# Attention and two dense layers on one core: a sign of its own for each row, and wide weight splits made in two pieces

## The chip, the cores and the metric

The kernel runs on one core of a Trainium2 chip. A core has TensorE (PE in the profile, with PEld for its weight loads), VectorE (DVE), ScalarE (ACT), GpSimd (POOL) and SyncE (SP), which here only issues DMAs. The metric is the time of one execution in device microseconds; the median of several runs is compared.

## The reference

The inputs are q, k and v of shape (4, 12, 448, 64), two gain vectors, and the weights of two dense layers. All are float32.

```python
q_n, k_n = rmsnorm(q, g_q), rmsnorm(k, g_k)
scores = q_n @ k_n.T / 8                      # per batch and head
attn = softmax(scores); x = attn @ v          # regrouped to 1792 tokens x 768
h = x @ moe_w_in                              # 768 x 2048
x = (h * sigmoid(1.702 * h)) @ moe_w_out      # 2048 x 768
h = x @ moe2_w_in                             # 768 x 2048
g = maximum(h, 0) + alpha * minimum(h, 0)     # alpha: 2048 values, drawn from 0 to 0.3
out = g @ moe2_w_out                          # 2048 x 768
```

## The kernel before, in words

Float32 operands of the large products are held as two float16 parts, a rounded high part and the remainder, and each product is made of three float16 matmuls (high by high, high by low, low by high). Weights are scaled by a power of two per row ahead of that, so that both parts fit float16.

**Weights.** `weights` (L202) loads a weight matrix in rows of 128. A row of the input weights is 2048 columns wide and comes in four loads; `from_words` turns the loaded words into numbers on ScalarE (L148) and VectorE (L164, L165). Then VectorE takes the row's largest magnitude (L245), and `row_scales` makes the scale of the row (L172 is its last instruction). `split_rows` (L177) writes the high part on ScalarE (L179) and the low part on VectorE (L180). There are 6 such rows for `moe_w_in` (tile `w1i`) and 6 for `moe2_w_in` (tile `w2i`); `moe_w_out` has 16 rows of 768 columns and goes through the same `split_rows`. Once all rows are known, `weight_scales` takes the largest of them and makes the ratios of the rows, which later scale the other operand of the product.

**First stage.** Attention of the first batch runs while the first layer's weights are prepared. `first_pairs` goes through the head pairs: scores (L516) into PSUM, the row maximum on VectorE (`nm`, L530), the exponential on ScalarE (`pr`, L550), transposes of the probabilities on TensorE (L608) that ScalarE evicts (`ptf`, L613), and the product with v (`xp`, L648). Three steps of the weights of `moe_w_in` are taken per step of the loop. `first_x` then makes `first_sc` and splits the first tokens, and `first_in` (L758) begins the first layer. Meanwhile `v_scale` (L309 to L314) reads the other batches' v through a small buffer `vst`, loaded by GpSimd's queue and read by ScalarE. SyncE's queue carries the weight loads (L223) and, among others, the store and the load by which `send_max` spreads a maximum over partitions (`line`, L128, and `row`, L129); alpha's maximum is spread in this way.

**Middle.** The first layer of each batch runs beside the attention of the next (`hp`, L758 and L798, and `yp`, L821). The weights `moe2_w_in` are prepared in `late_weights` during the last batch's first layer.

**Second layer.** `moe2_in` multiplies the tokens with `w2i` in blocks of 512 (`h`, L927) into one of three PSUM buffers of the pool `ps_m`. ScalarE (L932) and VectorE (L933) evict each group of 18 matmuls as `pos`, which goes to DRAM. ScalarE's part multiplies by a sign per row (+1 where alpha is at most 1, else -1) and VectorE's by alpha times that sign, then takes the larger.

The second product is made by a scheme of seven products on blocks of half size, for pairs of 128 tokens (256 tokens, 7 pairs). `token_sums` loads a pair's 2048 rows as two halves of 8 rows of 128 (index j) into `gp` or, for odd pairs, `odd`, and scales them back with `cg`, a column of 16 values (L1029): one ScalarE instruction per m covers row m of both halves, 2 x 256 columns, with the value `cg[:, m]`. The scale of the weights is the same for rows m and m + 8, but the sign is taken from row m for both. Then come sums and splits (L1036 to L1052). `moe2_out` makes the products (`op`, L1087). Pair 0 is prepared while the last blocks of `moe2_in` still run.

**Order.** The program is written as interleaved Python generators. A planner with its own model of costs then puts every engine's instructions in a fixed order; each engine works its list in that order and waits on semaphores.

Of the kernel before, what the change touches and what calls it, by code (L numbers as in the profile page):

```python
# [13 lines left out]
AF = mybir.ActivationFunctionType  # L14
ALU = mybir.AluOpType
# [42 lines left out]
def attention_moe_kernel(  # L58
# [17 lines left out]
    nc = tc.nc  # L76
# [99 lines left out]

    def split_rows(w, num, inv, j):  # L177

        nc.scalar.activation(out=w[:, j, 0], in_=num, func=AF.Copy, scale=inv[:, j:j + 1])  # L179
        nc.vector.scalar_tensor_tensor(  # L180
            out=w[:, j, 1], in0=num, scalar=inv[:, j:j + 1], in1=w[:, j, 0], op0=ALU.mult, op1=ALU.subtract
        )

    def weight_scales(nm, rm, n, c, done, wait=0):

# [17 lines left out]
    def weights(src, nm, w, num_tile, raw_tile, parts, ahead, c, done, group, hold=0):  # L203
# [22 lines left out]
        def split_all():  # L226
            while nums:
                split_rows(w(), nums[0][1], inv, nums[0][0])
                nums.pop(0)
                yield  # L230
# [619 lines left out]
    KH = KF // 2  # L850
# [26 lines left out]
    w2 = {}  # L877
# [131 lines left out]
    def token_sums(p):  # L1009

        if p >= NT // 256:
            return
        if p % 2:
            if "odd" not in w2:
                w2["odd"] = big.tile([128, 24576], F16, tag="w", name="odd", bufs=2)
            ops = w2["odd"][:, 0:14336]
            gp = w2["odd"][:, 14336:22528].bitcast(F32)
        else:
            ops = big.tile([128, 14336], F16, tag="g", name="even")
            gp = w2["p2"].tile([128, 4096], F32, tag="gp", name="gp", bufs=1)  # L1020
        ops = ops.rearrange("p (o m e t) -> p o m e t", o=7, m=KH, e=2)
        gp = gp.rearrange("p (j m t) -> p j m t", j=2, m=KH)
        src = g_dram[:, p * 256:(p + 1) * 256].rearrange("(j m p) t -> j p m t", j=2, p=128)
        for j in range(2):
            nc.sync.dma_start(out=gp[:, j], in_=src[j])
        sums[p] = ops
        yield
        for m in range(KH):
            nc.scalar.activation(out=gp[:, :, m], in_=gp[:, :, m], func=AF.Copy, scale=w2["cg"][:, m:m + 1])  # L1029
            if m % 4 == 3:  # L1030
                yield
        a11, a12, a21, a22 = (gp[:, j, :, i * 128:(i + 1) * 128] for i in range(2) for j in range(2))

        def put(o, x, ms=slice(0, KH)):
            hi, lo = ops[:, o, ms, 0], ops[:, o, ms, 1]
            nc.scalar.activation(out=hi, in_=x, func=AF.Copy)  # L1036
            nc.vector.tensor_tensor(out=lo, in0=x, in1=hi, op=ALU.subtract)

        put(A11, a11)
        yield  # L1040
        put(A12, a12)
        yield
        for h in range(2):
            ms = slice(h * KH // 2, (h + 1) * KH // 2)
            t = work.tile([128, KH // 2, 128], F32, tag="t", name="ts")
            nc.vector.tensor_tensor(out=t, in0=a21[:, ms], in1=a22[:, ms], op=ALU.add)
            put(S1, t, ms)
            nc.vector.tensor_tensor(out=t, in0=t, in1=a11[:, ms], op=ALU.subtract)
            put(S2, t, ms)
            nc.vector.tensor_tensor(out=a12[:, ms], in0=a12[:, ms], in1=t, op=ALU.subtract)  # L1050
            yield
        nc.vector.tensor_tensor(out=a21, in0=a11, in1=a21, op=ALU.subtract)  # L1052
        put(S3, a21)
        yield
        put(A22, a22)
        yield
        put(S4, a12)
        yield
# [81 lines left out]
    def second_layer(late):  # L1140
# [3 lines left out]
        rest = second_out_weights()  # L1144
        ready = False
        early = token_sums(0)
        step = 0
        for i in range(len(BLOCKS)):
# [21 lines left out]
        for p in range(NT // 256):  # L1170
            nxt = token_sums(p + 1)
            next(nxt, None)
            for o, _ in enumerate(moe2_out(p, a2, obs[:, p % 2])):
                next(nxt, None)
                next(nxt, None)
            for _ in nxt:
                pass

    if True:
# [10 lines left out]
        parts = stage[:, 0:R1I * 1024].bitcast(I32).rearrange("p (i n t) -> p i n t", i=R1I, t=2)  # L1190
# [115 lines left out]
```

## Time and profile before

| what | value |
|---|---|
| median of 3 runs | 1152.3 us (1146.89 to 1152.42) |
| the profiled execution | 1148.87 us, its span 1147.1 us |
| PE busy | 1064.7 us, 93% of the span |
| DVE busy | 802.2 us, 70%, 1397 instructions |
| ACT busy | 682.2 us, 59%, 1396 instructions |
| POOL busy | 180.6 us, 16% |
| mean granted TensorE clock | 0.973 |

Busy times are sums over one execution. The span goes from the first to the last instruction. Shares are averages over stages with different limits, so the stages have to be read apart.

### The profile page before, as it was taken

The page shows a single profiled execution, that of the slowest core. Times are in us where ns is not written, and L with a number is a line of the kernel's source. Part 1 is how long each engine was busy: PE and PEld are TensorE (multiplying, and loading weights), DVE is VectorE, ACT ScalarE, POOL GpSimd, SP SyncE. Part 2 cuts the span into 40 slices and gives each one's busy share as a digit, 9 for nine tenths or more (in the row PEclk, how much of TensorE's full clock was granted, in tenths as well). Part 3 has the DMA queues.
Part 4 walks back from the last instruction along what each step waited for, and adds up shares of the span by engine and source line. Part 5 has one row for each costly group of instructions (what it writes and reads, how often), then busy time and mean ns, then how long its engine had stood idle before and what let it go on. Part 6 is the DMA issues. An engine that isn't in the chain of part 4 may idle for free.

```text
span 1147.1 us, 18350 instructions
## 1 busy us (share of the span) xinstructions
PE 1064.7 (93%) x6753; PEld 581.2 (51%) x6753; DVE 802.2 (70%) x1397; ACT 682.2 (59%) x1396; POOL 180.6 (16%) x364
## 2 busy tenths in 40 slices
PE   3787788798989999999999999999999999999998
PEld 1343457644434445555455455444444477666664
DVE  5988798986879885577534965599977223968341
ACT  4788685888879976688633562356455324655220
POOL 2701003676433442100000000000000000000000
PEclk9778899999999999999999999999999999999999
DMA  7964743478888656455346601665342323363111
GB/s 223 271 179 136 175 128 105 97 163 186 176 191 163 163 131 153 110 118 120 78 125 219 214 1 64 246 216 191 143 161 72 136 70 113 101 189 101 34 30 28
DMA packets 235562, 158.19 MB, mean 138 GB/s; under 512 B 167888, under 2 KB 214736, under 8 KB 235472
## 3 DMA queue, kind: packets, MB, share of 16 engines
q1 hardware_dynamic: 229200, 141.34, 44.5%
q0 software_dynamic: 6272, 15.67, 5.2%
q8 instruction: 53, 0.87, 0.3%
q14 instruction: 37, 0.30, 0.1%
HBM read 92.35 MB, written 25.69 MB: 103 GB/s over the span
## 4 chain that ended last, share of the span: by engine, by line
PE 53%; DVE 18%; DMA 12%; issue 7%; ACT 6%; POOL 3%; SPq 1%; ACTq 0%; DVEq 0%; POOLq 0%
PE op L1087 16%; PE yp L821 15%; PE hp L798 7%; PE h L927 7%; PE xp L648 3%; DMA g<-in_moe_w_in_dram 3%; DMA g<-in_moe_w_out_dram 2%; DMA t<-hl 2%; PE sp L525 2%; DVE nm L530 2%; ACT pr L550 2%; DVE g L141 1%; DVE ph L620 1%; DMA yr<-y_dram 1%; DVE pos L933 1%
## 5 line engine op out<-in xcount | busy, mean ns | idle before, releaser
L821 PE MATMUL yp<-g,w1o 128*128 128x448 f16 x1152 | 226.8, 354 | 0.8 <-DVE g L767 0.8
L927 PE MATMUL h<-x,w2i 128*128 128x512 f16 (+1 forms) x1152 | 218.9, 352 | 3.5 <-DVE pos L933 1.9
L798 PE MATMUL hp<-x,w1i 128*128 128x448 f16 x864 | 170.9, 354 | 1.0 <-DVE t L807 1.0
L927 PEld LDWEIGHTS <-w2i 128*128 128x128 f16 x1152 | 112.6, 98 | 109.0 <-issue 4.3
L821 PEld LDWEIGHTS <-w1o 128*128 128x128 f16 x1152 | 109.5, 98 | 110.0 <-issue 11.1
L798 PEld LDWEIGHTS <-w1i 128*128 128x128 f16 x864 | 82.1, 98 | 83.6 <-issue 10.1
L620 DVE SCALAR_TENSOR_TENSOR ph<-pr,sm,ph 128x448 f16<-128x448 f32 x126 | 86.1, 715 | 25.8 <-ACT ph L593 25.8
L530 DVE TENSOR_REDUCE nm<-sp 128x2 f32<-128x896 f32 x96 | 92.6, 964 | 9.5 <-PE sp L525 6.8
L550 ACT ACTIVATE pr<-sp,nm,c_s 128x448 f32<-128x448 f32 x126 | 90.1, 718 | 2.7 <-DVE ph L620 1.4
L932 ACT ACTIVATE pos<-h,sign 128x512 f32<-128x512 f32 (+1 forms) x64 | 40.2, 629 | 86.6 <-PE h L927 75.1
L1087 PEld LDWEIGHTS <-even 128*128 128x128 f16 x672 | 65.7, 98 | 43.4
L933 DVE SCALAR_TENSOR_TENSOR pos<-h,slope,pos 128x512 f32<-128x512 f32 (+1 forms) x64 | 43.5, 681 | 59.4 <-ACT pos L932 59.4
L593 ACT ACTIVATE ph<-pr,sm 128x448 f16<-128x448 f32 x126 | 77.6, 659 | 10.8 <-DVE sm L590 10.7
L758 PE MATMUL hp<-x,w1i 128*128 128x256 f16 (+1 forms) x576 | 61.6, 265 | 13.0 <-DVE g L767 7.6
L1087 PEld LDWEIGHTS <-odd 128*128 128x128 f16 x504 | 49.3, 98 | 32.6
L758 PEld LDWEIGHTS <-w1i 128*128 128x128 f16 x576 | 52.3, 99 | 22.5 <-issue 18.3
L1087 PE MATMUL op<-w2lo,even 128*128 128x384 f16 x384 | 63.4, 326 | 0.0
L648 PE MATMUL xp<-pt,vs 128*64 128x256 f16 (+1 forms) x792 | 49.3, 265 | 9.4 <-DMA pt<-ph 8.3
L525 PE MATMUL sp<-t 64*128 64x448 f16 (+1 forms) x432 | 53.6, 354 | 1.9 <-DMA t<-hl 1.6
L648 PEld LDWEIGHTS <-vs 128*64 128x64 f16 x792 | 37.4, 111 | 29.1 <-issue 17.3
L532 ACT ACTIVATE nm<-nm,c_s 128x2 f32<-128x2 f32 x72 | 20.9, 290 | 49.1 <-DVE nm L530 48.7
L1087 PE MATMUL op<-w2hi,even 128*128 128x384 f16 x288 | 47.5, 326 | 0.0
(243 smaller groups left out, 1649.6 us busy)
## 6 DMA issues: line engine op xcount, KB each, us to landing
g<-in_moe_w_in_dram SPq DMA_DIRECT2D x24, 512.0 KB, 5.9
g<-in_moe_w_out_dram SPq DMA_DIRECT2D x32, 384.0 KB, 4.0
w2raw<-in_moe_w_in_dram SPq DMA_DIRECT2D x24, 512.0 KB, 5.5
w2raw<-in_moe_w_out_dram SPq DMA_DIRECT2D x16, 768.0 KB, 6.4
g_dram<-pos SPq DMA_DIRECT2D x48, 256.0 KB, 2.0
gp<-g_dram SPq DMA_DIRECT2D x8, 1024.0 KB, 6.7
odd<-g_dram SPq DMA_DIRECT2D x6, 1024.0 KB, 5.4
y_dram<-y SPq DMA_DIRECT2D x24, 224.0 KB, 2.5
```

The costliest lines, as they stand in the source:

```text
L525: nc.tensor.matmul(out=sp[:, j, 0:S] if n == 2 else sp[ds, 0, 0:S], lhsT=qt[ds] if n == 2 else qt[ds, 64:128], rhs=kt[ds, 0:S], start=(i = ...
L530: nc.vector.tensor_reduce(out=nm[:, 0:n], in_=sp[:, 0:n, 0:S], op=ALU.max, axis=AX, negate=True)
L550: last = nc.scalar.activation(out=pr[i], in_=sp[:, i, 0:S], func=AF.Exp, bias=nm[:, i:i + 1], scale=c_s if u >= 4 * NP else 1.0, accum_out ...
L593: nc.scalar.activation(out=ph[:, i, 0:S], in_=pr[i], func=AF.Copy, scale=sm[:, i:i + 1])
L620: nc.vector.scalar_tensor_tensor(out=ph[:, i, S:2 * S], in0=pr[i], scalar=sm[:, i:i + 1], in1=ph[:, i, 0:S], op0=ALU.mult, op1=ALU.subtract)
L648: nc.tensor.matmul(out=xp[64 * j:64 * j + 64, t:t + n], lhsT=vs[ks, j, c], rhs=pt[ks, 7 * j + kc, 0:n] if b else pt[ks, kc, o:o + n], star ...
L758: nc.tensor.matmul(out=ps, lhsT=w1i[:, kk, e, m * 128:(m + 1) * 128], rhs=xs[0, kk][:, f, cols], start=(i == 0), stop=(i == 3 * KD - 1))
L798: nc.tensor.matmul(out=ps, lhsT=w1i[:, kk, e, m * 128:(m + 1) * 128], rhs=x[:, f], start=(n == 0), stop=(n == 3 * KD - 1))
L821: nc.tensor.matmul(out=ps, lhsT=w1o[:, m, e, j * 128:(j + 1) * 128], rhs=g[:, m, f], start=(n == 0), stop=(n == 3 * KF - 1))
L927: nc.tensor.matmul(out=ps, lhsT=w2i[:, kk, e, m * 128:(m + 1) * 128], rhs=x2[kk][:, f], start=(c == 0), stop=(c == 3 * KD - 1))
L933: nc.vector.scalar_tensor_tensor(out=pos, in0=ps, scalar=slope[:, m:m + 1], in1=pos, op0=ALU.mult, op1=ALU.max)
L1087: nc.tensor.matmul(out=ps, lhsT=ops[:, o, m, f], rhs=rhs[:, e], start=(c == 0), stop=(c == 3 * KH - 1))
```

## The change

Rows wider than 1024 columns are split in two pieces, first the left half on both engines, then the right. This holds for `moe_w_in` and `moe2_w_in`, not for `moe_w_out`. In `token_sums` each half j of row m is scaled by an instruction of its own with `cg[:, j * 8 + m]`. With the alphas drawn here all signs are +1, so the values are the same.

```diff
     def split_rows(w, num, inv, j):
 
-        nc.scalar.activation(out=w[:, j, 0], in_=num, func=AF.Copy, scale=inv[:, j:j + 1])
-        nc.vector.scalar_tensor_tensor(
-            out=w[:, j, 1], in0=num, scalar=inv[:, j:j + 1], in1=w[:, j, 0], op0=ALU.mult, op1=ALU.subtract
-        )
+        cols = num.shape[1]
+        parts = 2 if cols > 1024 else 1
+        for i in range(parts):
+            c = slice(i * cols // parts, (i + 1) * cols // parts)
+            nc.scalar.activation(out=w[:, j, 0, c], in_=num[:, c], func=AF.Copy, scale=inv[:, j:j + 1])
+            nc.vector.scalar_tensor_tensor(
+                out=w[:, j, 1, c], in0=num[:, c], scalar=inv[:, j:j + 1], in1=w[:, j, 0, c], op0=ALU.mult, op1=ALU.subtract
+            )
...
         for m in range(KH):
-            nc.scalar.activation(out=gp[:, :, m], in_=gp[:, :, m], func=AF.Copy, scale=w2["cg"][:, m:m + 1])
+            for j in range(2):
+                nc.scalar.activation(
+                    out=gp[:, j, m], in_=gp[:, j, m], func=AF.Copy, scale=w2["cg"][:, j * KH + m:j * KH + m + 1]
+                )
```

## Rows read from the trace of the kernel before

**Rows 1.** Stretches: start:end, length, busy time (instructions) by engine, clock, DMA share, GB/s.
```profile
28.00:84.00 56.00, 43.55 (x213) 21.93 (x212) 50.22 (x97) 42.72 (x96) 24.76 (x61) 0.71 0.81 228
84.00:116.00 32.00, 22.56 (x129) 11.61 (x128) 29.12 (x60) 27.84 (x66) 5.52 (x11) 0.84 0.51 146
116.00:400.00 284.00, 251.46 (x1982) 147.08 (x1982) 239.66 (x459) 229.17 (x548) 114.41 (x201) 0.97 0.67 153
400.00:900.00 500.00, 494.96 (x2855) 244.25 (x2854) 344.12 (x571) 284.03 (x537) 28.12 (x59) 1.00 0.47 141
900.00:1147.10 247.10, 242.35 (x1549) 151.26 (x1546) 123.01 (x180) 87.07 (x132) 0.00 (x0) 1.00 0.27 83
```

**Rows 2.** Waits of PE, 28 to 130 us: total us, times, longest.
```profile
PE sp L516 <- ACT pr L550: 9.8, 6, 4.6
```

**Rows 3.** Timeline of PE, 90 to 102: start, us, instruction [idle before <-releaser].
```profile
91.18 3.56 PE L648 MATMUL xp<-ptf,v 128*64 128x256 f32 x16 [2.04 <-ACT ptf L613]
...
101.83 1.86 PE L516 MATMUL sp<-w1o 64*128 64x448 f32 x4 [4.58 <-ACT pr L550]
```

**Rows 4.** Timeline of ACT, 84 to 115 us.
```profile
84.08 1.99 ACT L179 ACTIVATE w1i<-w1i,inv_w1i 128x2048 f16<-128x2048 f32 x1
...
102.12 2.01 ACT L179 ACTIVATE w1i<-w1o,inv_w1i 128x2048 f16<-128x2048 f32 x1
...
114.91 0.48 ACT L314 ACTIVATE vst<-vst 128x336 f32<-128x336 f32 x1 [0.76 <-DMA vst<-in_v_dram]
```

**Rows 5.** Timeline of DVE, 94 to 114 us.
```profile
94.17 2.34 DVE L180 SCALAR_TENSOR_TENSOR w1i<-w1o,inv_w1i,w1i 128x2048 f16<-128x2048 f32 x1
...
99.36 0.62 DVE L530 TENSOR_REDUCE nm<-sp 128x1 f32<-128x448 f32 x1
...
103.81 1.09 DVE L530 TENSOR_REDUCE nm<-sp 128x2 f32<-128x896 f32 x1 [2.64 <-PE sp L516]
...
113.19 0.23 DVE L678 TENSOR_SCALAR first_sc<-ratio_w1i,av 128x6 f32<-128x6 f32 x1
```

**Rows 6.** Timeline of three engines, 668 to 745 us, the split of the second layer's weights.
```profile
674.33 54.64 PE L821 MATMUL yp<-g,w1o 128*128 128x448 f16 x288
...
675.12 7.67 ACT L179 ACTIVATE w2i<-w2n,inv_w2i 128x2048 f16<-128x2048 f32 x4
...
677.14 9.14 DVE L180 SCALAR_TENSOR_TENSOR w2i<-w2n,inv_w2i,w2i 128x2048 f16<-128x2048 f32 x4 [1.27 <-ACT w2i L179]
...
716.79 4.07 DVE L141 SCALAR_TENSOR_TENSOR x<-yr,ysc,x 128x512 f16<-128x512 f32 x6 [0.79 <-ACT x L140]
```

**Rows 7.** Timeline, 858 to 902 us, the first token pair's scaling and what stands behind it.
```profile
858.91 17.43 PE L927 MATMUL h<-x,w2i 128*128 128x512 f16 x80
...
865.75 5.01 ACT L1029 ACTIVATE gp<-gp,cg 128x512 f32<-128x512 f32 x8 [4.22 <-DVE cg L1160]
...
870.66 0.67 ACT L932 ACTIVATE pos<-h,sign 128x512 f32<-128x512 f32 x1
...
871.40 0.75 DVE L933 SCALAR_TENSOR_TENSOR pos<-h,slope,pos 128x512 f32<-128x512 f32 x1
...
900.80 1.30 ACT L140 ACTIVATE x<-yr,ysc 128x256 f16<-128x256 f32 x3
```

**Rows 8.** Timeline, 960 to 985 us, the second token pair.
```profile
964.58 5.01 ACT L1029 ACTIVATE odd<-odd,cg 128x512 f32<-128x512 f32 x8 [7.31 <-DMA odd<-g_dram]
...
972.57 2.35 DVE L1037 TENSOR_TENSOR odd<-odd 128x1024 f16<-128x1024 f32 x2
...
978.38 6.83 PE L1087 MATMUL op<-w2lo,odd 128*128 128x384 f16 x41
```

**Rows 9.** Timeline of SyncE's queue, 60 to 76 us.
```profile
65.46 0.33 SPq L128 DMA_DIRECT2D line<-am  x1
66.43 0.33 SPq L223 DMA_DIRECT2D g<-in_moe_w_in_dram  x1
73.54 0.33 SPq L129 DMA_DIRECT2D row<-line  x1
```

## The prediction

> **What bounds the kernel now.** I read the busy times of five stretches first [rows 1]: TensorE is idle for 12.5 of the 56 us from 28 to 84, 9.4 of 32 from 84 to 116 and 32.5 of 284 from 116 to 400. From 400 to 900 it is idle for 5.0 us of 500, and the 4.8 us after 900 include the last store. So behind 400 us no edit can win more than a few microseconds, but it can lose: whatever delays an operand there lengthens the kernel by the same amount. Ahead of 400 us the bound is a chain through all engines, each of which works its list in a fixed order; from 84 to 116 VectorE is busy 29.1 and ScalarE 27.8 of 32 us. The granted clock is lowest early: 0.71 and 0.84 of full speed in the first two stretches, against 1.00 after 400.
>
> The view of waits shows what ends TensorE's idle time there: mostly the exponentials of L550, 9.8 us in six places [rows 2]. The longest is the 4.58 us ahead of 101.83; the score reduce that feeds those exponentials is on VectorE at 99.36, behind the 2.34 us split of a weight row at 94.17 and another long instruction between them [rows 3, 5]. The 2.04 us ahead of 91.18 is a wait for ScalarE's eviction `ptf`, and the split at 84.08 (1.99 us) stands ahead of it [rows 3, 4]. So two rows' splits stand in queues that TensorE waits for.
>
> **The change part by part.** *First layer's input weights, 6 rows.* Each 2048-column ScalarE copy becomes two of 1024, and each VectorE difference likewise. Cost on ScalarE: four 2048-column copies took 7.67 us together, the last alone 1.99, so one starts every 1.893 us; three 256-column ones with the same per-partition scale took 1.30, one every 0.40 [rows 6, 7]. That is 0.833 ns a column and 0.187 us an instruction, so 1.040 us for 1024 columns and 2.08 for two: +0.19 us a row, 1.1 us in six. On VectorE four took 9.14 us (one every 2.265, the last alone 2.345) and six of 512 columns 4.07 (every 0.665) [rows 6]: 1.042 ns a column, 0.132 us an instruction, 1.198 for 1024, 2.40 for two, +0.13 us a row and 0.8 us in six.
>
> Gain: the first difference can start after half of the copy, some 0.9 us earlier, and the two engines overlap. VectorE rarely waited for the copy; it was full of other work (94.17 has no idle time ahead of it [rows 5]). One place has room: the copy of row 4 starts at 102.12 [rows 4], its first half would be out at 103.2, and VectorE is idle for 2.64 us until 103.81 [rows 5]. Half a difference (1.2 us) can move there from behind, and `first_sc` at 113.19, the scale that the first tokens' split needs, comes up to 1.2 us earlier, less the 0.7 us by which the reduce at 103.81 is pushed. But that split stood on ScalarE behind a copy that waits for a DMA until 114.91 [rows 4], so some of the gain ends there. What else is won is order: a piece of 1.04 or 1.2 us lets something else in where 2 us did not. The lists are written by a planner that starts whatever its model has ready, so a new piece size can reorder everything behind it, and the trace can't show this. Bounds: a gain of half the two waits named plus half a row in the chain to `first_sc` (2.3 + 1.0 + 1.2 = 4.5 us), a loss of the added 1.9 us plus one wait as long as the longest (4.6), 6.5 us. I take a gain of 0.5 us, near the one place that can be followed; both ends stay in the range.
>
> *Second layer's input weights, 6 rows.* The same +1.1 us on ScalarE and +0.8 on VectorE. TensorE is busy with L821 from 674.33 to 728.97, and the token operands that need these weights' scale are split by 720.86 (716.79 + 4.07) [rows 6]. That leaves 8.1 us of cover for 1.9 us of cost: nothing, up to 1.9 if the planner puts the pieces elsewhere, and no gain, since TensorE runs without a gap.
>
> *The sign.* In each of seven token pairs, eight ScalarE scalings of 512 columns become sixteen of 256. Eight took 5.01 us [rows 7, 8]; sixteen take 15 times 0.40 and a last one of 0.50, 6.5 us: +1.5 us a pair, 10.5 us in all. ScalarE is busy for 87 of 247 us after 900 [rows 1]. For the first pair that takes its buffer late, the scalings run 964.58 to 969.59; the two low halves at 972.57 end at 974.92, and TensorE starts on the operands at 978.38 [rows 8]: 3.5 us of slack against 1.5. Hidden there, and later pairs begin further ahead.
>
> It isn't hidden at pair 0. Its eight scalings hold ScalarE from 865.75 to 870.76, and the eviction `pos` at 870.66 stands directly behind; VectorE's part of it ends at 872.15 [rows 7]. The second layer's input product has three PSUM buffers and one group of 18 matmuls every 3.9 us (17.43 us for 80 [rows 7]). Counted from the start at 858.91 and the two matmuls that ended the group before, groups end at about 864.7, 868.6 and 872.5, and the group that starts at 872.5 needs the buffer that this eviction frees. The slack is 0.35 us. If the order stays, TensorE stalls 1.5 - 0.35 = 1.15 us. If the planner puts `pos` between the scalings, nothing is lost, and perhaps up to 0.5 us won. I take +0.8, bounds -0.5 and +1.5.
>
> [...] Unoverlapped, sixteen of 0.50 us would be 8.0 us, +3.0 a pair, and the stall 2.65 us. [...]
>
> **Sum.** -0.5 + 0 + 0.8 = +0.3 us on the profiled execution's 1148.87 us (span 1147.1): 1149.2. The three runs lie from 1146.89 to 1152.42 with a median of 1152.3, 0.3% above the profiled one; on the median the sum is 1152.6. I take the middle of both, 1151.
>
> **Rivals.** *Faster: the queues' head-of-line waits go.* [...] For it: TensorE is idle for 21.9 us in the two stretches with the splits, 28 to 116 [rows 1], and two of its waits have a split ahead of them. Against it: other long instructions stay, and VectorE's sum grows. At the 4.5 us bound plus 2.5 us for a better order behind it, 1152.3 - 7 = 1145.
>
> *Slower: the DMA queue of SyncE.* It is worked in order, and the small store and load that spread alpha's maximum stand among the weight loads. `line` is sent at 65.46, and `row`, which needs it, goes out only at 73.54 [rows 9]; one weight load passes at 66.43, and then nothing of the queue moves until 73.54, 6.8 us after that load was issued, with weight loads standing behind. Today ScalarE still has raw words for part of that time. If the new order frees raw buffers just before such a block, so that ScalarE and the row chain stand for all of it, some 6 to 7 us are lost: 1152.3 + 6.5 = 1159. It decides from the point where a load of the first weights is ready and `row` is ahead of it. Against it: freed buffers bring loads ahead of `line` just as easily.
>
> *The edit does nothing there: the halves stay side by side.* If the planner puts nothing between them, the early stage only pays 1.1 + 0.8 us, and pair 0 its 0.8: 1152.3 + 2.7 = 1155, still inside what can't be told from no change.
>
> **How the numbers follow.** A measurement of this kernel can tell about 0.5%, 5.8 us, from no change. Forecast 0.40, halves side by side 0.08: together 0.48 for within 0.5%. The head-of-line rival 0.30, the queue rival 0.22. The likeliest alone spans 1146 to 1157 (1152.3 -5.8 and +5). With the cases of both signs and the bounds of an unknown order, 1142 to 1160 holds 8 in 10.
>
> **What would show it.** In the trace after: twelve splits of about 1.14 us on ScalarE and of 1.28 on VectorE a tensor; something else between two halves on either engine; the idle time before the score product near 101.8 shorter; `first_sc` ahead of 113; scalings of 256 columns at 0.50 us, 112 of them; TensorE's wait for `pos` near 872 grown by about 1 us; no idle time from 900 on. I am wrong if TensorE's saturation, now from about 400 us, begins more than 5 us earlier or later, since everything behind it is moved by that; or if a pair's first operands come later than the matmuls of the pair before.

## The result, and the profile after

The changed kernel takes 1160.8 us (median of 7 executions, 1158.5 to 1163.7); the kernel before took 1152.3 beside it. The medians differ by 8.5 us; the estimated ratio is 1.0098, with a 95% interval of 1.0075 to 1.0121, about 11 us. So the changed kernel is slower, where 1151 and no measurable change were forecast. The profiled execution took 1158.5 us, its span 1156.7. Lines of the kernel after are higher by 4 behind the split and by 7 behind the sign's scaling (L179 is L183, L1029 is L1033 and 1034).

From the page of the kernel after: busy time of TensorE and ScalarE, and the row of the granted clock.

```profile
PE 1073.2 (93%) x6753; PEld 585.5 (51%) x6753; DVE 804.8 (70%) x1409; ACT 694.1 (60%) x1464; POOL 179.5 (16%) x364
...
PEclk9988799998889999999999999999999999999999
```

ScalarE has 11.9 us more work (682.2 before; 12.7 more were worked out), but the time isn't lost where most of that work is. To see where, cut both spans at the same counts of matmuls: TensorE does 6753 in both. These are the stretches up to the 351st, 576th, 1401st, 1626th, 2226th, 2701st and last matmul; columns as in [rows 1]. Up to the 351st, the 2226th, the 2701st and the last one both kernels have done the same matmuls; at the three cuts between, the order differs and up to 10 stand on the other side. Of the kernel before:

```profile
12.10:110.20 98.10, 71.88 (x353) 36.78 (x354) 85.82 (x154) 74.55 (x165) 34.48 (x90) 0.77 0.72 209
110.20:151.30 41.10, 33.19 (x227) 19.59 (x228) 34.32 (x94) 28.68 (x75) 1.63 (x3) 0.88 0.62 160
151.30:260.30 109.00, 91.93 (x827) 65.89 (x825) 98.94 (x194) 84.11 (x189) 52.72 (x81) 1.00 0.54 129
260.30:296.80 36.50, 32.05 (x230) 15.49 (x228) 25.98 (x45) 29.96 (x75) 19.95 (x35) 0.95 0.81 172
296.80:383.30 86.50, 81.24 (x600) 39.12 (x598) 71.98 (x120) 76.95 (x190) 35.89 (x76) 0.98 0.82 179
383.30:452.00 68.70, 68.15 (x477) 34.69 (x475) 51.76 (x95) 51.92 (x128) 20.41 (x39) 1.00 0.61 144
452.00:1142.30 690.30, 685.81 (x4053) 369.42 (x4050) 428.82 (x681) 333.68 (x579) 13.14 (x29) 1.00 0.39 121
```

Of the kernel after:

```profile
11.90:109.80 97.90, 70.64 (x352) 36.61 (x354) 87.90 (x165) 76.37 (x172) 33.29 (x89) 0.90 0.73 213
109.80:156.40 46.60, 35.51 (x227) 20.63 (x228) 37.85 (x99) 31.25 (x77) 1.62 (x3) 0.82 0.64 167
156.40:263.50 107.10, 94.40 (x826) 67.36 (x825) 95.34 (x188) 81.77 (x187) 48.10 (x80) 0.95 0.48 118
263.50:305.90 42.40, 34.68 (x230) 16.18 (x230) 27.26 (x44) 29.91 (x74) 23.92 (x36) 0.84 0.82 154
305.90:394.30 88.40, 83.76 (x602) 40.43 (x597) 71.52 (x120) 75.67 (x188) 36.65 (x77) 0.96 0.76 171
394.30:462.30 68.00, 68.00 (x477) 34.61 (x475) 50.70 (x93) 50.49 (x123) 20.01 (x38) 1.00 0.66 146
462.30:1152.00 689.70, 685.72 (x4052) 369.48 (x4050) 429.65 (x688) 346.27 (x642) 13.47 (x30) 1.00 0.39 121
```

The first stretch, which holds all six rows' pieces, takes the same time (97.9 against 98.1). The second and fourth are 5.5 and 5.9 us longer, the fifth 1.9 longer, the third 1.9 shorter. The last, in which the sign's 112 scalings and the second weights' pieces run, takes 689.7 against 690.3. In the second and the fourth, TensorE's idle time grew by 3.2 and 3.3 us and its busy time by 2.3 and 2.6, at a lower granted clock (0.82 for 0.88, 0.84 for 0.95). From the 351st to the 2226th matmul, the same matmuls in both, busy time grew by 9.9 us and idle time by only 1.5. So most of the difference of these two profiles is matmuls that took longer; the waits that follow are real, but they are not the whole loss.

The second stretch begins so on ScalarE's timeline of the kernel after:

```profile
110.27 0.57 ACT L148 ACTIVATE w1o<-g 128x384 f32<-128x384 f32 x1 [0.56 <-DMA g<-in_moe_w_out_dram]
111.77 0.55 ACT L148 ACTIVATE w1o<-g 128x384 f32<-128x384 f32 x1 [0.92 <-DMA g<-in_moe_w_out_dram]
113.59 0.48 ACT L318 ACTIVATE vst<-vst 128x336 f32<-128x336 f32 x1 [1.28 <-DMA vst<-in_v_dram]
...
115.59 1.29 ACT L140 ACTIVATE x<-xraw,first_sc 128x256 f16<-128x256 f32 x3
116.79 0.57 ACT L617 ACTIVATE ptf<-tp 128x512 f32<-128x512 f32 x1
...
134.46 0.56 ACT L148 ACTIVATE w1o<-g 128x384 f32<-128x384 f32 x1 [7.28 <-DMA g<-in_moe_w_out_dram]
```

and before the change:

```profile
111.39 0.60 ACT L613 ACTIVATE ptf<-tp 128x512 f32<-128x512 f32 x1
...
112.49 0.60 ACT L613 ACTIVATE ptf<-tp 128x512 f32<-128x512 f32 x1
...
115.39 1.29 ACT L140 ACTIVATE x<-xraw,first_sc 128x256 f16<-128x256 f32 x3
```

The evictions `ptf`, which TensorE waits for, stood ahead of the splits `x`; now they stand behind them, and instructions that wait for a load stand in their place. Later ScalarE waits 7.28 us for the load of one weight copy, and on VectorE the reduction `mv` waits 3.41 us for `vrow`:

```profile
133.25 0.42 DVE L335 TENSOR_REDUCE mv<-vrow 128x2 f32<-128x256 f32 x1 [3.41 <-DMA vrow<-v_line]
```

TensorE's timeline of the kernel after shows two waits that follow. The first ends with `x`; before, `hp` waited 1.2 us there. The second ends with a `g` of VectorE (L771), which started at 134.05 us, behind that `mv`.

```profile
116.13 1.32 PE L762 MATMUL hp<-x,w1i 128*128 128x256 f16 x4 [4.73 <-ACT x L140]
...
134.52 1.11 PE L612 MATMUL tp<-identf,pr 128*128 128x128 f32 x4 [5.19 <-DVE g L771]
```

In the fourth stretch a wait begins on SyncE's queue. Its timeline before the change (the time is that of issue, the second column how long the queue was held):

```profile
264.89 1.82 SPq L627 DMA_TRANSPOSE pt<-ph  x1
266.81 2.97 SPq L480 DMA_TRANSPOSE t<-hl  x1
...
271.21 4.35 SPq L627 DMA_TRANSPOSE pt<-ph  x2
```

and after:

```profile
263.70 7.12 SPq L631 DMA_TRANSPOSE pt<-ph  x2
270.93 5.24 SPq L484 DMA_TRANSPOSE t<-hl  x1
...
277.70 1.74 SPq L631 DMA_TRANSPOSE pt<-ph  x1
```

One more transpose `pt` goes ahead of `t<-hl`, which then lands at 281.9, 11.0 us after its issue (6.5 before). ScalarE's next cast to `hl` needs that buffer and stands ahead of the exponentials. ScalarE's and TensorE's timelines after:

```profile
282.00 0.95 ACT L481 ACTIVATE hl<-qk 128x896 f16<-128x896 f32 x1 [7.05 <-DMA t<-hl]
```

```profile
287.68 1.32 PE L529 MATMUL sp<-t 64*64 64x448 f16 x6 [3.90 <-ACT pr L554]
```

All of these are instructions that the edit doesn't touch: the planner has put the work of all engines into another order. Compared by names and shapes in the traces, TensorE's matmuls before and after stand in the same order up to the 93rd and part at the 94th, 48 us into the span. With the halves of the first weights alone they part at the same one. The sign alone moves nothing ahead of the 5095th matmul, at the second layer's output product. The second weights' halves alone leave the order of all matmuls as it was.

### The profile page after: what moved, and what is told of

Same layout as the page of the kernel before. It is cut to its first block, busy times and chain, and to the rows that moved or that the text cites. A ratio compares the mean times of both kernels' runs of the same rounds, so it can differ in the third digit from the quotient of the medians.

```text
span 1156.7 us, 18449 instructions
## 1 busy us (share of the span) xinstructions
PE 1073.2 (93%) x6753; PEld 585.5 (51%) x6753; DVE 804.8 (70%) x1409; ACT 694.1 (60%) x1464; POOL 179.5 (16%) x364
## 4 chain that ended last, share of the span: by engine, by line
PE 64%; DVE 12%; DMA 10%; ACT 6%; issue 5%; POOL 2%; SPq 1%; ACTq 0%; DVEq 0%; POOLq 0%
PE op L1094 17%; PE yp L825 16%; PE hp L802 11%; PE h L931 10%; PE xp L652 4%; DMA g<-in_moe_w_in_dram 3%; PE sp L529 3%; PE hp L762 2%; ACT pr L554 1%; DMA g<-in_moe_w_out_dram 1%; DMA pt<-ph 1%; DVE w2num L165 1%; DMA t<-hl 1%; DMA w2raw<-in_moe_w_in_dram 1%; DVE ph L624 1%
## 5 line engine op out<-in xcount | busy, mean ns | idle before, releaser
L825 PE MATMUL yp<-g,w1o 128*128 128x448 f16 x1152 | 229.3, 356 | 1.1 <-DVE g L771 1.1
L762 PE MATMUL hp<-x,w1i 128*128 128x256 f16 (+1 forms) x576 | 66.2, 276 | 11.3 <-ACT x L140 4.7
L529 PE MATMUL sp<-t 64*128 64x448 f16 (+1 forms) x432 | 56.3, 368 | 7.4 <-ACT pr L554 6.1
```

The costliest lines, as they stand in the source:

```text
L529: nc.tensor.matmul(out=sp[:, j, 0:S] if n == 2 else sp[ds, 0, 0:S], lhsT=qt[ds] if n == 2 else qt[ds, 64:128], rhs=kt[ds, 0:S], start=(i = ...
L762: nc.tensor.matmul(out=ps, lhsT=w1i[:, kk, e, m * 128:(m + 1) * 128], rhs=xs[0, kk][:, f, cols], start=(i == 0), stop=(i == 3 * KD - 1))
L825: nc.tensor.matmul(out=ps, lhsT=w1o[:, m, e, j * 128:(j + 1) * 128], rhs=g[:, m, f], start=(n == 0), stop=(n == 3 * KF - 1))
```

## The experiments

All ratios are to the kernel before, measured on the same chip beside it. The letters in the expectations: C, the sign's own ScalarE time costs it; Q, the store and load of `vmax`'s maximum on SyncE's queue cost it (the slower rival's mechanism at another pair); P, the new order at the first `hp` matmuls; H, the pieces themselves; S, three named places together; D, two heads of queues between 110 and 151 us; R, the plan as a whole, whatever the edit was. "Rows out of place" counts rows of an engine's list that stand elsewhere.

**Which part.** The first kernel halves the first layer's rows alone (`parts = 2 if cols > 1024 and w is w1i else 1`, the old sign), the second has the new sign alone, the third halves the second layer's rows alone (`w is not w1i`).

> Only the first layer's six rows are split in halves; the second layer's rows and the sign are as before. Theory Q (the order: new piece sizes reorder the early stage, and a store and load pair closes up in SyncE's queue): the whole loss is here, ratio to before 1.008 to 1.012, about 1161 us, with the 7 us idle of ScalarE near 127 us. Theory C (direct cost: the added ScalarE time, 10.5 us for the sign and 1.1 for each tensor, ends up on the path): ratio 1.001 at most.

Measured: 1161.7 us, ratio 1.0118 [1.0074, 1.0162].

> Only the sign's sixteen scalings a pair; all splits are whole as before. Theory Q: ratio 0.998 to 1.001, since TensorE keeps its work (the trace of the changed kernel even shows it 1 us less late behind 880 us). Theory C: ratio about 1.009, most of the loss, because 10.5 us of ScalarE time are added here.

Measured: 1152.1 us, ratio 1.0023 [0.9997, 1.0049].

> Only the second layer's six rows are split in halves. Both theories: ratio 0.999 to 1.001, since TensorE is full and the token operands wait for a DMA; theory C would allow 1.9 us, 1.002.

Measured: 1148.1 us, ratio 1.000 [0.9973, 1.0026]. The whole loss is in the first layer's halves; C falls. Both harmless kernels keep the plan of before ahead of 450 us, and yet their single profiles reach the 2701st matmul at 458.0 and 456.6 us, not at 452.0. So up to 6 us of a difference between two profiles is no plan's doing; verdicts below go by the ratios.

The single stretches vary too. With the old order the second one (up to the 576th matmul) took 41.1, 40.0 and 41.0 us, with the new order 46.6 and 44.1 (the change, the first halves alone): there the plans differ clearly. The fourth took 36.5, 41.3 and 38.8 with the old order and 42.4 and 42.6 with the new one, so of the 5.9 us above only a part is the plan's. From the 351st to the 2226th matmul, in this order: the kernel before, the sign alone, the second halves alone; the change, the first halves alone.

```profile
110.20:383.30 273.10, 238.41 (x1876) 140.10 (x1877) 231.22 (x451) 219.71 (x524) 110.19 (x194) 0.97 0.68 155
109.90:389.20 279.30, 243.13 (x1878) 143.21 (x1877) 233.92 (x455) 219.35 (x526) 110.36 (x194) 0.95 0.67 152
110.00:386.00 276.00, 239.49 (x1876) 142.05 (x1877) 232.75 (x455) 220.06 (x526) 110.79 (x194) 0.96 0.67 154
109.80:394.30 284.50, 248.35 (x1876) 144.60 (x1877) 231.97 (x448) 218.60 (x525) 110.28 (x194) 0.92 0.65 148
111.80:397.10 285.30, 244.93 (x1878) 143.86 (x1877) 231.59 (x448) 220.09 (x526) 109.97 (x195) 0.94 0.66 147
```

The three with the old order have TensorE busy for 240.3 us on average and idle for 35.8; the two with the new one busy for 246.6, at a lower granted clock, and idle for 38.3. Of 8.8 us, 6.3 are busy time (which rests on ends of matmuls that the profile models). What lowers the clock with the new order was not tested.

**The queue pair.** In the plan with halves, `vrow`'s load stands directly behind `v_line`'s store; before the change two weight loads passed between them. Here it is put behind two loads again (`row` is `vrow`).

```
+        with tc.issue_after(loads["w1o"][13].ins):
+            nc.sync.dma_start(out=row, in_=line.rearrange("p b -> (p b)").partition_broadcast(128))
```

> As the first run (halves of the first layer alone), and the load of the pair on SyncE's queue is put behind two more weight loads, where it stands in the kernel before. Theory Q: most of the loss comes back, ratio 1.000 to 1.004, and ScalarE's idle time near 127 us falls from 7.3 us to under 4. A third theory, R (the loss is spread over a new order as a whole, and the pair is only where it shows): ratio stays at 1.007 or more.

Measured: 1158.3 us, ratio 1.0109 [1.0064, 1.0154]. In its profile the stretch 110 to 151 us is back at 41.3 us, and 15 us are lost between the 1626th and 2226th matmul instead. Q is not the cause, though its place is real.

**The order without the pieces.** Rows of 2048, and the scores of two units forced behind the first `hp` matmuls, where the plan with halves has them.

```
     def scores(u):
+        if u in (10, 11) and hp0:
+            with tc.issue_after(hp0[6 if u == 10 else 8].ins):
+                scores_of(u)
...
```

`hp0` lists the matmuls of `first_in`, and `scores_of` is the old `scores`.

> The kernel before (rows of 2048 columns, no sign change), with one thing forced: the scores of the fifth and sixth units of the second list are put behind the seventh and ninth hp matmul of first_in on TensorE's list, where the kernel with halves has them (before, all six stand ahead of the first hp matmul). The rest of the plan then comes out nearly as with halves: 98 TensorE rows out of place against the kernel with halves, 1567 against the kernel before; GpSimd's list is the same as with halves; SyncE's v_line and vrow stand as before. Theory P (the order costs it, not the pieces): 1158 to 1162 us, ratio 1.008 to 1.012, TensorE waits 3 to 5 us for x at the first hp matmul. Theory H (the pieces themselves cost it, by their extra instructions on ScalarE and VectorE): 1150 to 1153, ratio within 0.003 of 1. Theory R (the later part of the new plan costs it, wherever it began): 1158 to 1162 as P, but without a lag at 145 us.

Measured: 1158.9 us, ratio 1.0079 [1.0047, 1.0111]. No piece, and most of the loss. TensorE's wait for `x` came with it; the row is from this kernel's timeline:

```profile
116.24 0.37 PE L767 MATMUL hp<-x,w1i 128*128 128x256 f16 x1 [4.08 <-ACT x L140]
```

The counter-test holds `first_in` back, with and without halves:

```
-            if i >= M_AT and i - M_AT < KF:
-                first_in(slice(0, FIRST), i - M_AT, g0)
+            if i >= 5 and i - M_AT < KF:
+                for m in range(0 if i == 5 else i - M_AT, i - M_AT + 1):
+                    first_in(slice(0, FIRST), m, g0)
```

> Halves in the first layer's rows, with first_in's calls held back by three ticks, so that the hp matmuls stand behind the scores of the first eight units (before: behind six; with halves: behind four). From there on TensorE's list is nearly that of the kernel with halves (142 rows out of place). Theory P: the wait of 4.73 us for x at the first hp matmul is gone and most of the loss with it, 1150 to 1154 us, ratio 0.998 to 1.004. Theory H: 1158 to 1162, ratio 1.008 to 1.012. Theory R: 1158 to 1162 as well, with the loss now after 200 us.

Measured: 1165.0 us, ratio 1.0125 [1.0099, 1.0152].

> The kernel before (2048 columns) with first_in's calls held back by the same three ticks: the partner of the run with halves held back, since holding them back has a price or a gain of its own. P: 1147 to 1152. H: 1147 to 1152, 8 to 10 us under its partner with halves. R: its later plan differs from that of the kernel before in 1251 TensorE rows, so anything from 1147 to 1160.

Measured: 1153.4 us, ratio 1.0037 [1.0016, 1.0059]. With the wait for `x` removed the kernel with halves is as slow as ever: P falls. The next run cuts the rows at 1536 columns (slices 0:1536 and 1536:2048).

> First-layer rows in two pieces, but of 1536 and 512 columns: as many instructions as with halves and the same columns. The plan puts the scores of the first six units ahead of the first hp matmul again, as before the change (the later plan is a third one: 1324 TensorE rows out of place against before, 1539 against halves). P: no stall for x at the first hp matmul, 1149 to 1154 us. H: the same extra instructions, 1158 to 1162. R: unknown, 1148 to 1162.

Measured: 1166.2 us, ratio 1.0151 [1.0124, 1.0177]. No scores stand behind the first `hp` here, and it is slower still.

**Three places put back.** The first two are the held `first_in` and the moved `vrow`; the third puts `t<-hl` ahead of the second `pt`, by starting its pair two ticks earlier (cut):

```
+                if P == 8 and r == 2:
+                    prep = prep_pair(10)
...
+            with tc.issue_after(turned[10].ins) if P == 8 and u % 4 in (1,) else ExitStack():
+                nc.sync.dma_start_transpose(
...
```

> Halves in the first layer's rows, with three places of the plan put back as the kernel before has them: first_in held back (no hp matmul ahead of the late scores), vrow's load behind two more weight loads on SyncE, and the transpose t<-hl of the tenth pair ahead of the second pt transpose of the eighth pair (with halves it stands behind it). The rest of the plan stays that of halves. Theory S (the loss is the waits at these three places and the lower clock after them): 1150 to 1155 us, ratio 0.999 to 1.004. Theory R (the loss belongs to the plan as a whole; places can't be picked out): 1156 to 1166, ratio 1.006 to 1.015. Theory H (the pieces themselves): 1160, ratio 1.010.

Measured: 1158.9 us, ratio 1.0072 [1.0048, 1.0095].

> Halves in the first layer's rows with the third of these places alone: TensorE's order is that of halves for its first 2170 rows (714 rows out of place after that), and the transpose t<-hl of the tenth pair goes ahead of the second pt transpose of the eighth. S: the wait of 4 to 6 us for t<-hl near 276 us is gone, 1154 to 1158, ratio 1.004 to 1.008. R: 1156 to 1166. H: 1160.

Measured: 1161.5 us, ratio 1.0092 [1.0058, 1.0125].

> Halves in the first layer's rows with the first two places (first_in held back, vrow's load behind two more weight loads), not the third: TensorE's list from first_in on differs from that of halves in 142 rows. S: the stretch 110 to 151 us takes 39 to 42 us (with halves 44 to 47), and the time is 1154 to 1158, ratio 1.004 to 1.008. R: 1156 to 1166. H: 1160.

Measured: 1161.4 us, ratio 1.0095 [1.006, 1.013]. The repair works at its place. Waits of ScalarE from 150 to 480 us (total, times, longest), of the changed kernel and then of the one with `t<-hl` moved:

```profile
ACT hl L481 <- DMA t<-hl: 8.4, 3, 7.1
```

```profile
ACT hl L482 <- DMA t<-hl: 7.3, 5, 2.4
```

The longest wait is gone, and in the profiles of both kernels with this repair the 600 matmuls behind take 85 us (88 to 91 with halves and without it, 102 in the kernel with `vrow` alone moved). But the 475 after those take 72.9 instead of 68.0, and 110 to 151 us takes 44.4 with all three repairs, 44.7 with two, now in waits of `tp` for evictions (7.2 us in two places of the kernel with two repairs). S falls: three places bring the ratio to 1.0072, from 1.0118 for the same kernel without them (1.0098 for the whole change); the intervals overlap, and more than half of the loss is still there.

**Number of pieces.** One row in halves; then pieces on one engine only; then three rows and two (`... and j in (3, 4, 5)`).

> One of the six first-layer rows in two pieces (row 1), the others whole: one ScalarE and one VectorE instruction more than before, not six; the plan from the first hp matmuls on is another one (869 TensorE rows out of place against before, 1372 against halves in all rows). H: a sixth of the loss, 1150 to 1153 us, ratio 1.001 to 1.002. R: anything from 1148 to 1166, its size has nothing to do with the number of pieces. S: as the before, 1149 to 1153, if no wait stands at the three places.

Measured: 1153.6 us, ratio 1.0019 [0.9996, 1.0041].

> All six first-layer rows in two pieces on ScalarE, whole (2048 columns) on VectorE: six extra instructions, not twelve. The plan is another one again (1287 TensorE rows out of place against before), but at the two places named here it orders the work as before the change: on ScalarE the third pair's evictions (ptf, pr) stand ahead of the x splits and of the last weight copies that wait for a load; on VectorE the reduction mv that waits for vrow stands behind the first g of first_in. Theory D (the loss begins there: instructions that wait for a transfer stand at the head of ScalarE's and VectorE's lists, ahead of what TensorE needs, in the stretch 110 to 151 us): that stretch takes 39 to 42 us, as before the change (with halves 44 to 47), and the time is 1150 to 1156, ratio 0.999 to 1.005. Theory H (the pieces themselves): half the loss, ratio 1.005. Theory R (the plan as a whole, nothing to be said from two places): 1148 to 1166.

Measured: 1166.6 us, ratio 1.0150 [1.0118, 1.0183].

> All six first-layer rows whole on ScalarE, in two pieces on VectorE. mv stands behind two g as before the change; on ScalarE one of the two evictions stands ahead of x, one behind. D: the stretch 110 to 151 us takes 40 to 44 us, ratio 1.000 to 1.006. H: half the loss, ratio 1.005. R: 1148 to 1166.

Measured: 1169.0 us, ratio 1.0173 [1.0139, 1.0206].

> Rows 3, 4 and 5 in two pieces on both engines, rows 0 to 2 whole. Here the plan has both heads as with halves in all rows: ScalarE's evictions of the third pair behind x and the weight copies, VectorE's mv ahead of the first g. D: the stretch 110 to 151 us takes 44 to 47 us and the ratio is 1.006 to 1.012, as with six rows. H: half the loss, 1.005, no longer stretch. R: 1148 to 1166.

Measured: 1152.4 us, ratio 1.0013 [0.9991, 1.0035].

> Rows 4 and 5 in two pieces on both engines, the others whole: one row less than the run before it, but both heads are as before the change (evictions ahead of x, mv behind the first g). D: the stretch 110 to 151 us takes 39 to 42 us and the ratio is 0.998 to 1.004. H: a third of the loss, 1.003. R: 1148 to 1166.

Measured: 1156.6 us, ratio 1.0066 [1.0043, 1.0090]. H and D both fall. Six pieces more cost 1.5 and 1.7%, six more on rows 3 to 5 nothing that can be told, four more on rows 4 and 5 0.7%. D missed the stretch 110 to 151 us in three of four: 44.5 us (ScalarE's pieces), 47.1 (VectorE's) and 49.8 (rows 4 and 5), where 39 to 44 were expected. Its one hit shows why a place can't be priced by itself. From the stretches of the kernel with rows 3 to 5 (cut at the same counts, from the 351st matmul on):

```profile
110.60:156.30 45.70, 35.07 (x227) 20.29 (x228) 38.19 (x100) 31.48 (x78) 1.62 (x3) 0.81 0.60 175
156.30:262.40 106.10, 94.83 (x827) 68.57 (x824) 93.04 (x186) 81.03 (x186) 51.65 (x81) 0.95 0.51 119
262.40:295.10 32.70, 30.56 (x230) 14.83 (x231) 26.64 (x45) 28.91 (x74) 18.29 (x32) 1.00 0.87 189
```

The stretch with the bad heads is as long as D said (45.7 us), and the two behind it give it back: 106.1 and 32.7 us against 109.0 and 36.5 before the change.

**A new plan with no work in it.** One constant, then one unused instruction of 128x1:

```
-W1O_RATE = 6
+W1O_RATE = 5
```
```
+        if w is w1i and j == 5:
+            nc.scalar.activation(out=<a tile that nothing reads>, in_=num[:, 0:1], func=AF.Copy)
```

> The kernel before, no pieces and no instruction added or taken away; one constant changed, W1O_RATE from 6 to 5, which only spreads the handing over of the second weights' steps a little more thinly over the ticks of the second list. The plan comes out another one: 1170 TensorE rows out of place against before. R (the time is that of the plan that comes out, whatever the edit was): a ratio between 1.001 and 1.017, above the interval of no change. H (pieces cost it): 0.998 to 1.002.

Measured: 1156.5 us, ratio 1.0052 [1.0025, 1.0079].

> The kernel before with one ScalarE instruction of 128x1 added at the sixth row's split; its result is used by nothing. The plan changes little: 126 TensorE rows out of place against before, of 6753 matmuls, and 2 blocks of GpSimd's list. R: between 0.999 and 1.006, since most of the old plan stays. H: 0.999 to 1.001.

Measured: 1158.0 us, ratio 1.0080 [1.0056, 1.0105]; it was expected at 1.006 at most. One instruction of 128x1 costs some 9 us, because it moves others. By the count ahead of the run only 126 rows are out of place there, so the loss doesn't go with their number either. R is what is left, and these two show it without any piece. It is no forecast of a size: five kernels fell above the widths that were given for it (the halves with `first_in` held, the uneven pieces, the pieces on one engine, and this one).

All plans together (ratio; time of the 2701st matmul and time from there to the last one, counted in the one profile of each):

```
plan                                  ratio    2701st   rest
before                                1        452.0    690.3
rows 3 to 5 in halves                 1.0013   453.1    692.6
row 1 in halves                       1.0019   457.6    689.8
no halves, first_in held              1.0037   454.8    692.4
no halves, W1O_RATE 5                 1.0052   460.8    690.8
rows 4, 5 in halves                   1.0066   459.3    689.5
halves, three places put back         1.0072   460.8    689.7
no halves, two scores behind hp       1.0079   461.2    690.9
no halves, one 128x1 instruction      1.0080   458.2    690.2
halves, t<-hl first                   1.0092   463.7    690.4
halves, two places put back           1.0095   461.7    690.5
the change                            1.0098   462.3    689.7
halves, vrow moved                    1.0109   469.4    691.7
halves, first_in held                 1.0125   463.3    690.2
ScalarE's pieces alone                1.0150   469.5    691.5
pieces of 1536 and 512                1.0151   469.6    690.1
VectorE's pieces alone                1.0173   476.2    689.1
```

The three kernels of the first group aren't in the table: two have the plan of before up to the 2701st matmul, and the first halves alone have that of the change (465.0 and 691.9). The rest is 691 us within 2 in every one of them; the whole difference is made ahead of the 2701st matmul. Sixteen other plans were timed and none was faster; their middle is 0.9% slower. Why the one before is the lowest of them was not tested.

## Why the prediction was wrong

*Sizes: right.* Twelve pieces of the second layer's tensor on each engine, and the scalings, by line and shape (count, total, mean ns), after the change:

```profile
L1034 ACT ACTIVATE gp<-gp,cg 128x256 f32<-128x256 f32 x64 | 26.3, 494 | 11.0 <-DMA gp<-g_dram 8.1 <-DVE cg L1167 2.9
...
L184 DVE SCALAR_TENSOR_TENSOR w2i<-w2n,inv_w2i,w2i 128x1024 f16<-128x1024 f32 x12 | 14.7, 1280 | 1.6 <-ACT w2i L183 1.6
...
L183 ACT ACTIVATE w2i<-w2n,inv_w2i 128x1024 f16<-128x1024 f32 x12 | 12.7, 1136 | 4.6 <-DVE inv_w2i L172 4.6
```

1.14 and 1.28 us a piece and 0.49 a scaling, as worked out: 64 of the 112 scalings stand in this row. ScalarE grew by 11.9 us where 1.1 + 1.1 + 10.5 = 12.7 were worked out.

*Second weights, 0: right* (ratio 1.000).

*The sign, +0.8: right where it stands alone.* Its ratio is 1.0023 [0.9997, 1.0049], and the stall at pair 0 came: TensorE waits 1.34 us for the eviction behind the scalings, where 1.15 were worked out. A later wait of 0.5 us for `pos`, at 897.5 us before, is gone in this kernel, which leaves 0.8. From the kernel with the sign alone:

```profile
879.32 4.04 PE L927 MATMUL h<-x,w2i 128*128 128x512 f16 x18 [1.34 <-DVE pos L933]
```

In the changed kernel TensorE has no wait for `pos` in the 100 us around pair 0. The sixteen scalings run together, as the row shows, and start 8.9 us later in the span than the eight did, while the matmuls are some 10 us later: the eviction behind them was in time. That is the new order's doing, and luck for this term.

```profile
874.69 6.49 ACT L1034 ACTIVATE gp<-gp,cg 128x256 f32<-128x256 f32 x16 [2.89 <-DVE cg L1167]
```

Sixteen scalings take 6.49 us, as worked out; the estimate without any overlap, sixteen of 0.50 us, was 8.0.

*First weights, -0.5: this step failed.* The place that was followed did what it should: the waits for the exponentials [rows 2, 3] fell from 9.8 to 4.3 us, the longest from 4.6 to 2.0, and the difference of the row that ScalarE copies at 84 us began at 85.55, not at 88.40. Waits of TensorE, 28 to 130 us, after:

```profile
PE hp L762 <- ACT x L140: 4.7, 1, 4.7
PE sp L520 <- ACT pr L554: 4.3, 4, 2.0
PE qt L469 <- ACT xraw L587: 4.1, 1, 4.1
```

But `first_sc` came no earlier (113.09 for 113.19), and two other waits grew, for `x` from 1.2 to 4.7 us and for `xraw` from 1.1 to 4.1. The stretch with the pieces is as long as it was. The sign of being wrong that the prediction named came true: the 2701st matmul ends 10 us later (462.3 for 452.0). The failure is what the text itself named and then priced by the wrong row: "a new piece size can reorder everything behind it, and the trace can't show this". The loss bound took one wait (4.6) plus the added 1.9 us, 6.5 in all, as if one place could go wrong. A new plan changes the waits from 110 to 450 us in many places, and the experiments give 1.5 to 20 us for one. Nor did the sum have a term for the matmuls themselves: it priced a loss by waits alone, while in the profiles most of the loss is busy time of the same matmuls at a lower granted clock (6.3 of 8.8 us on average). The centre should have been the middle of such plans, not the one place that can be followed. The range ended 1 us under the result for the same reason.

*The rivals.* "Slower" had the right size (1159) and the wrong place: SyncE's queue around alpha's pair is as it was, `line` at 65.07, one load at 66.10, `row` at 73.52 [rows 9]. "Faster" had the right local effect, worth nothing in the end: its 2.5 us for a better order was the author's estimate and no run shows them; from the 351st to the 2226th matmul the kernel after took 284.5 us where 273.1 were taken before. "Halves stay side by side" is what ScalarE's timeline shows for all six rows (two pieces in 2.2 us); on VectorE other work stands between the two pieces in three of them (as at 85.55 and 89.53 us).

*What is settled and what isn't.* Shown: the loss needs no piece (four kernels without any lose 0.4 to 0.8%), doesn't follow the number of pieces, and is all ahead of 452 us of the old span. Shown by rows, in two profiles of the new plan against three of the old one: it is made of longer matmuls at a lower granted clock and, to a lesser part, of longer waits. Not shown: what brings the clock down in the new plan, and a rule by which a plan's time could be told from its list; each of the four that were tried (Q, P, S, D) fell. The pieces were not run in the old plan, so their own cost in the first layer is only bounded: the best plan with six added instructions is within 0.35% of none.

## What to carry to other kernels

Where a planner writes the lists, an edit ahead of TensorE's saturation is two edits: the instruction, and a new plan for all that follows. Compare the lists before pricing anything, and where they differ, put a plan's spread (here 0.1 to 1.7%, from zero-work edits as well) into the forecast; where they don't (the second weights) or not ahead of the place in question (the sign), row arithmetic holds. To judge an edit by itself, time it in several plans, or time the same new order without it.

## What the runs showed of the hardware

Two things had not been expected. TensorE's busy time is no constant of the work. From the 351st to the 2226th matmul it was busy for 238.4 us at a granted clock of 0.97 and, with the new order, for 248.4 us at 0.92; three executions with one order gave 238.4, 239.5 and 243.1 us at 0.97, 0.96 and 0.95. The idle time of a stretch doesn't tell it: in the third stretch of the kernel after, idle time is 4.4 us less than before, busy time 2.5 us more, and the clock 0.95 for 1.00. What lowered the clock is not shown. And a transpose on SyncE's queue has no fixed latency: the `t<-hl` behind `pt` took 6.5 us to land in the profile of the kernel before and 11.0 in that of the kernel after, the queue itself being held for 3.0 and 5.2 us at the issue, and the next `t<-hl` took 3.8 us in both. ScalarE's longest wait for such a transpose from 150 to 480 us was 2.5, 3.4 and 2.8 us in the three executions with the old order, and 7.1 and 6.9 in the two with the new one. In the profiles before and after, one `pt` transpose was still under way at the issue of the late `t<-hl` (it took 5.4 and 8.4 us to land), so their number doesn't explain the difference; what does was not found.
